# Where the first chunks' attention lands: weight places lent to batches 0 and 1, PSUM banks of its own, and two tiles summed by VectorE

## The chip, the cores and the metric

The kernel runs on 1 core of one Trainium2 chip. The metric is device time in microseconds (us), the median of the runs shown. PE is TensorE, ACT is ScalarE, DVE is VectorE, POOL is GpSimd, and SP is the queue that issues nearly all DMA transfers.

## The reference

Attention over keys and values that are averaged in groups of 8 rows, and a feed-forward block on its output:

```python
k_p = k.reshape(B, H, Sp, pool, D).mean(axis=3)      # B=8, H=8, S=576, D=64, pool=8, Sp=72
v_p = v.reshape(B, H, Sp, pool, D).mean(axis=3)
scores = scale * q @ k_p.T ; scores -= max ; attn = exp(scores) / (sum + 1e-9)
x = (attn @ v_p)  ->  (4608, 512)
h = x @ w_in                                         # 512 -> 2048
g = h * erf(softplus(h))
out = g @ w_out                                      # 2048 -> 512
```

The activations are float32, the two weight matrices arrive as float64 and are used at float32 precision.

## The kernel before, in words

**Tiling.** The 4608 tokens are cut into 9 chunks of 512 tokens. A chunk's feed-forward block goes in 16 steps, one for each 128 of the 2048 hidden units. A step has an input GEMM (L584, 12 matmuls of 128x512) and an output GEMM (L631, 12 more). Every float32 operand is held as a high and a low half (names ending in h and l), and a product is the sum of three: high by high, high by low, low by high. Steps go in pairs: two input GEMMs into two PSUM banks of the kind "h", then softplus (L602) of both, Erf (L609) of both with an activation table load ahead of each, the product with h on VectorE (L612), the split into halves gh (L614) and gl (L617), and later the output GEMMs. For chunk 0, L612 is what frees the "h" banks; the next pair's input GEMMs need them.

**Attention.** A tile is 128 tokens (64 at a batch's end) of all 8 heads. Batch 0 fills chunk 0 with four tiles, and its last 64 tokens begin chunk 1; batch 1 follows. The keys (DMA, L383) are summed over the pool by VectorE for batches 0 and 1 (L386), and by POOL for the others (L389 to L393), and split into kbd (L402, L404); the values go into vah, val and vb (L412 to L424). For each tile: queries land (L436), are split into qh and ql (L309 or L310, L442), scores (L476, or L452 and L454 from chunk 2 on and for full tiles), the maximum by head (L481 or L463), exponential, sums z, reciprocal (L505, L507), scaling (L517), transposes (L524, L531), split into eth, etl and etb (L528, L529, L536 to L541), and for each block of up to 256 tokens the products with the values (L561) and the split of their result into xh and xl (L565, L567), the input GEMM's operands.

The exponential is a sigmoid far down its tail. In chunk 0 ScalarE takes it head by head straight from PSUM, with the sum accumulated (L491, 8 for a tile), after VectorE has scaled the negated maximum (L484). In the other chunks VectorE subtracts the maximum (L465, L497), ScalarE takes one sigmoid over the 576 numbers of a row (L501), and VectorE sums them (L503).

**Weights.** They stay on the chip: 16 pieces of w_in (wi0 to wi15) and 16 of w_out (wo0 to wo15), each 512 KB from HBM (L345). A piece is converted from float64: ScalarE scales the upper word into a PSUM bank of the kind "cv" (L348), the lower bits come from ScalarE or POOL (L353, L355), VectorE puts them together (L357, L359), and the result is split (L309 or L310, L364).

**What sets the order.** Every operation is recorded with an engine, a cost, a due time and the buffers that it reads and writes. A planner (`Program.order`) then places them one by one: it keeps a clock for each engine, and takes of all ready operations within a window of due times the one that can start first, with a bonus for an early due time. Buffers have a number of places by tag (two of "raw" for landing keys, values and queries, two "h" banks, four "o", four "att", two "cv", eight banks in all), and an operation can be taken only when places for its buffers are free by the planner's clock. The instructions of each engine then stand in the order in which they were taken, and each engine works through its own in that order. SP's queue too goes in order: a transfer that waits for its place holds the ones behind it. Where the planner expects TensorE to be idle in the first 57 us of its clock, it puts filler matmuls on the constants (L675), which keep TensorE busy.

Of the kernel before, what the change touches and what calls it, by code (L numbers as in the profile page):

```python
# [122 lines left out]
class Program:  # L123
# [8 lines left out]
    DELAY = {"PE": 200, "ACT": 160, "DVE": 200, "POOL": 160, "SP": 900}  # L132
    SAME = {"PE": 0, "ACT": 130, "DVE": 130, "POOL": 105, "SP": 0}

    def __init__(self, capacity, window):
        self.ops, self.capacity, self.window, self.filler = [], capacity, window, None

    def op(self, eng, cost, prio, fn, reads=(), writes=(), hold=(), alt=None, funcs=None, port=False):
# [4 lines left out]
        o.set, o.port = funcs, port  # L143
# [124 lines left out]
def moe_attention(ctx: ExitStack, tc: tile.TileContext, cst, qa, kl, vl, wi, wo, out):  # L268
# [13 lines left out]
    sizes.update({"banks": 8, "h": CAP_H, "o": CAP_O, "att": CAP_ATT, "cv": CAP_CV})  # L282
# [90 lines left out]
    def job(ck, b, tiles, off, times, first, fresh):  # L373

        base, due = times[0], times[-1] + VAL_R
        if fresh:
# [19 lines left out]
            for p in range(NP):  # L396
                load_pool(kl[b, p], ks, p, SP, base + KEYS + KEYS_R * p, "s" if first and p > 1 else "raw")
# [318 lines left out]
```

## Time and profile before

| | us |
|---|---|
| median of 3 runs | 950.01 (949.89 to 951.83) |
| the profiled execution | 949.92 |
| its span, first to last instruction | 948.0 |
| PE busy | 928.0 |
| ACT busy | 653.7 |
| DVE busy | 531.9 |
| POOL busy | 348.0 |

The profiled execution's time is 1.9 us more than its span. A busy PE is not a PE with useful work: the filler matmuls count as busy. In the rows of the timeline a row gives the start, the duration, the engine, the line, the operation, what is written and read, and in brackets how long the engine had been idle before it and what ended that.

### The profile page before, as it was taken

To read this page: it belongs to the slowest core of one execution; us is meant where nothing else is said; L and a number is where in the kernel's file an instruction comes from. 1 tells how busy PE (TensorE), PEld (TensorE's weight loads), DVE (VectorE), ACT (ScalarE), POOL (GpSimd) and SP (SyncE) were. 2 spreads that over 40 slices of the span, in tenths; PEclk is the share of its full clock that TensorE was granted. 3 is DMA by queue.
4 is the path that set the end of the run, shared out by engine and by line. 5 is a ranking of instruction groups with operands and counts; after the bars stand their busy time and mean duration, and the time that the engine had idled before them with its cause. 6 is when DMAs were issued, how large, how long until landed. Compare 5 with 4: busy or idle time off the path is not lost.

```text
span 948.0 us, 13049 instructions
## 1 busy us (share of the span) xinstructions
PE 928.0 (98%) x4636; PEld 771.9 (81%) x4636; DVE 531.9 (56%) x1021; ACT 653.7 (69%) x1131; POOL 348.0 (37%) x451
## 2 busy tenths in 40 slices
PE   7899989999999999999999999999999999999998
PEld 6778868888888888888888888888888888888886
DVE  6978686755565454555565655655476446423232
ACT  4789985867676767766676667766676667656664
POOL 3689986243322354235321452234342111101000
PEclk9999999999999999999999999999999999999999
DMA  8990112212111121111110122002210010001001
GB/s 322 363 357 7 37 36 70 77 38 62 39 45 36 38 67 45 45 43 47 51 67 13 37 68 78 23 14 59 68 56 23 1 45 1 1 1 44 1 1 45
DMA packets 30352, 58.58 MB, mean 62 GB/s; under 512 B 7120, under 2 KB 7248, under 8 KB 30288
## 3 DMA queue, kind: packets, MB, share of 16 engines
q1 hardware_dynamic: 30000, 57.23, 18.1%
q8 instruction: 37, 0.61, 0.3%
q10 hardware_dynamic: 288, 0.52, 0.1%
q14 instruction: 27, 0.22, 0.1%
HBM read 48.30 MB, written 9.44 MB: 61 GB/s over the span
## 4 chain that ended last, share of the span: by engine, by line
PE 84%; DVE 1%; ACT 0%; POOL 0%; issue 0%; POOLq 0%
PE banks L631 38%; PE banks L584 37%; PE banks L561 4%; PE banks L452 2%; PE banks L524 1%; PE banks L454 1%; PE banks L476 1%; PE banks L531 0%; DVE kbd L404 0%; DVE z L503 0%; ACT L501 0%; DVE hs L612 0%; ACT y L602 0%; DVE z L505 0%; DVE s L517 0%; ACT s L501 0%
## 5 line engine op out<-in xcount | busy, mean ns | idle before, releaser
L584 PE MATMUL banks<-xh,wi 128*128 128x512 f32 x1152 | 381.2, 393 | 3.5 <-DVE y L612 2.8
L631 PE MATMUL banks<-wo,gh 128*128 128x512 f32 x1152 | 363.2, 396 | 0.8 <-DVE etl L529 0.7
L584 PEld LDWEIGHTS banks<-xh,wi 128*128 128x128 f32 x1152 | 217.1, 188 | 51.1 <-DVE y L612 4.4
L631 PEld LDWEIGHTS banks<-wo,gh 128*128 128x128 f32 x1152 | 207.5, 188 | 39.6 <-DVE etl L529 1.1
L631 PE MATMUL banks<-wo,gl 128*128 128x512 f32 x576 | 225.3, 391 | 0.0
L584 PE MATMUL banks<-xl,wi 128*128 128x512 f32 x576 | 225.1, 391 | 0.0
L617 DVE TENSOR_TENSOR gl<-hs,gh 128x512 fp32r<-128x512 f32 x73 | 53.6, 736 | 157.4 <-ACT gh L614 153.3
L617 POOL TENSOR_TENSOR gl<-hs,gh 128x512 fp32r<-128x512 f32 x55 | 71.4, 1298 | 175.2 <-ACT gh L614 174.6
L631 PEld LDWEIGHTS banks<-wo,gl 128*128 128x128 f32 x576 | 108.1, 188 | 24.2 <-DVE gl L617 0.4
L590 ACT COPY hs<-banks 128x512 f32<-128x512 f32 x56 | 32.8, 586 | 136.2 <-PE banks L584 133.3
L584 PEld LDWEIGHTS banks<-xl,wi 128*128 128x128 f32 x576 | 108.6, 188 | 21.8
L614 ACT CAST gh<-hs 128x512 fp32r<-128x512 f32 x128 | 78.4, 614 | 35.5 <-PE banks L631 31.3
L589 DVE COPY hs<-banks 128x512 f32<-128x512 f32 x72 | 49.8, 692 | 92.1 <-PE banks L584 91.7
L602 ACT ACT_TABLE_LOAD x72 | 92.4, 1283 | 3.0 <-DVE gl L617 1.8
L612 DVE TENSOR_TENSOR hs<-y,hs 128x512 f32<-128x512 f32 x128 | 84.1, 697 | 15.2 <-ACT y L609 15.1
L609 ACT ACT_TABLE_LOAD x68 | 87.2, 1283 | 1.2
L442 POOL TENSOR_TENSOR ql<-raw,qh 128x512 fp32r<-128x512 f32 (+1 forms) x36 | 44.4, 1232 | 106.4 <-ACT qh L309 106.2
L609 ACT ACTIVATE y<-y 128x1024 f32<-128x1024 f32 (+1 forms) x73 | 76.4, 1048 | 0.8
L389 POOL TENSOR_TENSOR raw<-raw 128x256 f32<-128x256 f32 (+1 forms) x60 | 50.9, 849 | 70.5 <-DMA raw<-vl 40.8
L602 ACT ACTIVATE y<-hs 128x512 f32<-128x512 f32 x128 | 73.8, 624 | 0.7
L541 POOL TENSOR_SCALAR etb<-etb 32x256 fp32r<-32x256 f32 (+1 forms) x40 | 18.3, 458 | 88.8 <-ACT etb L536 54.8
L501 ACT ACTIVATE s<-s,cst 128x576 f32<-128x576 f32 (+1 forms) x36 | 27.9, 775 | 30.3 <-DVE s L465 30.2
(100 smaller groups left out, 1194.4 us busy)
## 6 DMA issues: line engine op xcount, KB each, us to landing
raw<-vl SPq DMA_DIRECT2D x42, 256.0 KB, 2.7
out<-f SPq DMA_DIRECT2D x34, 256.0 KB, 2.0
raw<-kl SPq DMA_DIRECT2D x30, 288.0 KB, 2.8
wi<-wi SPq DMA_DIRECT2D x16, 512.0 KB, 6.8
wo<-wo SPq DMA_DIRECT2D x16, 512.0 KB, 6.8
raw<-qa SPq DMA_DIRECT2D x28, 256.0 KB, 2.6
hs<-qa SPq DMA_DIRECT2D x4, 256.0 KB, 5.1
raw<-qa SPq DMA_DIRECT2D x8, 128.0 KB, 2.5
```

The source lines that it names most:

```text
L389: op("POOL", gps(4 * size), prio, lambda: nc.gpsimd.tensor_add(t.ap[:, 0:4], t.ap[:, 0:4], t.ap[:, 4:8]), [t], [t])
L442: e.tensor_sub(ql.ap[:, :, :T], raw.ap[:, :, :T], f32(qh.ap[:, :, :T]))
L561: nc.tensor.matmul(d, w, e, start=(i == 0), stop=(i == 3), skip_group_check=True)
L584: nc.tensor.matmul(ph.ap, w_in[ft].ap[:, w, P * p:P * p + P], x.ap[:, p, :], start=(p == 0 and q == 0), stop=(p == NP - 1 and q == 2))
L589: op("DVE", dve(TC), n + u + 1.2, lambda u=u, ph=ph: nc.vector.tensor_copy(hs[u].ap, ph.ap), [ph], [hs[u]], alt=("ACT", act(TC, True), lam ...
L590: [ph], [hs[u]], alt=("ACT", act(TC, True), lambda u=u, ph=ph: nc.scalar.copy(hs[u].ap, ph.ap)))
L602: nc.scalar.activation(y.ap[:, half(k)], hh[k].ap, AF.Softplus)
L609: op("ACT", act(w), n + 1.9, lambda sl=sl: nc.scalar.activation(y.ap[:, sl], y.ap[:, sl], AF.Erf), own, own, funcs="sigmoid")
L612: op("DVE", dve(TC), n + 1.9, lambda k=k: nc.vector.tensor_mul(g(k), y.ap[:, half(k)], hh[k].ap), [(y, k), hh[k]], [gs[k]], port=kept)
L614: op("ACT", act(TC), n + 2.0, lambda k=k: nc.scalar.copy(gh[k].ap, g(k)), [gs[k]], [gh[k]])
L617: e.tensor_sub(gl[k].ap, g(k), f32(gh[k].ap))
L631: nc.tensor.matmul(o[t].ap, g.ap[:, gs], w_out[ft].ap[:, w], start=(ft == 0 and q == 0), stop=(ft == NJ - 1 and q == 2))
```

## The change

It has these parts:

- Buffers of the first attention work may lie in the places of weight pieces that are not loaded yet (`loan`). Lent are: to the exponentials eth, etl and etb of chunk 0's second block the places of wo15, wo14 and wo13; to qh and ql of every second tile of chunk 0 those of wi15 and wo12; to the four key pieces of batch 1 those of wo8 to wo11, and to its six value pieces those of wi9 to wi14. The transfer of a weight piece is recorded with the loans of its place, and the planner takes it only when all of them have been read (`o.after`).
- PSUM banks of chunk 0's attention count against a limit of their own ("att0", 5) and no longer against the four of "att".
- Which of a tile's two groups of heads takes the exponential by head on ScalarE is a table. Chunk 0's first two tiles now go the other way for both groups: subtraction, one sigmoid, and the sum by VectorE.
- The planner's numbers are others: costs of operations, delays, due times of batches, weights and values, the window, the bonus.

```diff
-WINDOW = 10
-SHIFT = 4
+WINDOW = 12
+SHIFT = 3
-T0, T0_STEP = -10.5, 1.0
-VAL_R = 3.5
-KEYS, KEYS_R, KEYS_S = -5.5, 0.5, -1.0
-VALS, VALS_R, VALS_S = -2.0, 0.5, -1.2
+T0, T0_STEP = -10.5, 1.5
+VAL_R = 3.0
+KEYS, KEYS_R, KEYS_S = -7.5, 0.5, -1.0
+VALS, VALS_R, VALS_S = 0.0, 0.4, -1.2
-W_IN, W_OUT = -1.0, -2.0
-LEAD = 9
+W_IN, W_OUT = 2.0, 0.0
+LEAD = 4
-CAP_H, CAP_O, CAP_ATT, CAP_CV = 2, 4, 4, 2
-ON_ACT = (0,)
+CAP_H, CAP_O, CAP_ATT, CAP_CV, CAP_ATT0 = 2, 4, 4, 2, 5
+ON_ACT = ((0, 0), (0, 0), (1, 1), (1, 1))
+
+LENT_E = ("wo15", "wo14", "wo13")
+LENT_Q = ("wi15", "wo12")
+LENT_KV = ("wo8", "wo9", "wo10", "wo11", "wi9", "wi10", "wi11", "wi12", "wi13", "wi14")
-SLACK, BIAS = 30, 2000
+SLACK, BIAS = 50, 2000
-DGE = 1200
+DGE = 2000
...
-                    if o.prio > progress + self.window:
+                    if o.prio > progress + self.window or any(b.left for b in o.after):
...
-        return 0.84 * n + (160 if psum else 190)
+        return 0.84 * n + (90 if psum else 130)
-        return 1.15 * (n + 66) / 0.96
+        return 1.04 * n + 95
-        return 2.5 * n + 110
+        return 2.25 * n + 130
...
+    def loan(tag, shape, dtype=F32):
+
+        b = Buf(weights, [P] + shape, dtype, tag, [tag])
+        pr.loans.setdefault(tag, []).append(b)
+        return b
...
-            op("SP", 1350, due - LEAD, lambda: nc.sync.dma_start(raw.ap.rearrange("p f w -> p (f w)"), src), [], [raw])
+            op("SP", 1290, due - LEAD, lambda: nc.sync.dma_start(raw.ap.rearrange("p f w -> p (f w)"), src),
+               [], [raw]).after = pr.loans.setdefault(w.args[3], [])
...
-                t = buf(tag, [size, POOL] if on_dve else [POOL, size])
+                t = (loan if tag in LENT_KV else buf)(tag, [size, POOL] if on_dve else [POOL, size])
...
-        eth, etl, etb = buf("eth", [NP, 256], F32R), buf("etl", [NP, 256], F32R), buf("etb", [2, 256], F32R)
+        second = ck == 0 and off > 0 and wide
+        eth, etl, etb = (loan(LENT_E[i], sh, F32R) if second else buf(t, sh, F32R) for i, (t, sh) in
+                         enumerate((("eth", [NP, 256]), ("etl", [NP, 256]), ("etb", [2, 256]))))
+        bank = lambda kind: Buf(banks, [P, 512], F32, "banks", ["banks", "att0" if ck == 0 else kind])
...
-            raw, qh, ql = buf("hs" if first else "raw", [NP, P]), buf("qh", [NP, P], F32R), buf("ql", [NP, P], F32R)
+            raw, qh, ql = (buf("hs" if ck == 0 else "raw", [NP, P]), *(
+                loan(LENT_Q[i], [NP, P], F32R) if ck == 0 and off + at & P and wide else buf(t, [NP, P], F32R)
+                for i, t in enumerate(("qh", "ql"))))
...
+                on_act = ck == 0 and ON_ACT[(off + at) // P][g]
...
-            if not on_act:
+
+            left = [g for g in range(2) if not (ck == 0 and ON_ACT[(off + at) // P][g])]
+            if left:
```

How this moves instructions is seen at three places. In the rows, names are those of the buffers; L numbers of the change are 10 to 25 higher for the same operation.

First, SP's queue where the keys of batch 1 and the first weight pieces stand. kl are keys, vl values, qa queries, wi and wo weights. Before:

```order
L436 DMA hs<-qa 128x512
L383 DMA gl<-vl 128x512
L383 DMA gh<-vl 128x512
L345 DMA wi_240<-wi 128x1024
L345 DMA wi_247<-wi 128x1024
L345 DMA wi_296<-wi 128x1024
L345 DMA wi_311<-wi 128x1024
L383 DMA raw<-kl 128x576
L345 DMA wi_330<-wi 128x1024
L345 DMA wo_382<-wo 128x1024
L383 DMA raw<-kl 128x576 x2
```

In the change:

```order
L453 DMA hs<-qa 128x512
L395 DMA gh<-vl 128x512
L395 DMA wo_274<-kl 128x576
L395 DMA wo_280<-kl 128x576
L395 DMA wo_286<-kl 128x576
L395 DMA wo_289<-kl 128x576
L453 DMA raw<-qa 128x4x64
L356 DMA wi_298<-wi 128x1024
L453 DMA raw<-qa 128x512
L356 DMA wi_357<-wi 128x1024
L395 DMA wi_390<-vl 128x512
L395 DMA wi_404<-vl 128x512
```

The four key pieces of batch 1 went from behind four weight pieces to ahead of all, into the places of wo8 to wo11; the queries of the 64-row tile and of batch 1's first tile now stand around the first weight piece, where they stood ten and twenty transfers further back.

Second, ScalarE around the softplus of the first pair of steps (L602, L626 in the change). Before:

```order
L536 CAST etb<-banks 32x64 x2
L602 ACT_TABLE_LOAD
L602 ACTIVATE y<-banks 128x512 x2
L528 CAST eth<-banks 128x4x64
L309 ACTIVATE wo_877<-f 128x512
L348 ACTIVATE banks<-wo_460 128x512
L609 ACT_TABLE_LOAD
L609 ACTIVATE y<-y 128x1024
```

In the change:

```order
L524 ACTIVATE s<-s,cst 128x576
L365 ACTIVATE hs<-wi_520,cst 128x512
L552 CAST eth<-banks 128x4x64
L360 ACTIVATE banks<-wo_506 128x512
L626 ACT_TABLE_LOAD
L626 ACTIVATE y<-banks 128x512 x2
L589 CAST xh<-banks 128x64 x2
L633 ACT_TABLE_LOAD
L633 ACTIVATE y<-y 128x1024
```

The 64-row tile's copy (eth) moved ahead of the softplus, and the copy of a converted weight piece out of the stretch between softplus and Erf.

Third, ScalarE around the softplus of steps 12 and 13 of chunk 0. Before (wo_1055, wo_1082 are the pieces wo13 and wo14):

```order
L458 COPY s<-banks 128x144
L353 ACTIVATE hs<-wo_1082,cst 128x512
L353 ACTIVATE hs<-wo_1099,cst 128x512
L458 COPY s<-banks 128x144 x2
L309 ACTIVATE wo_1796<-f 128x512
L348 ACTIVATE banks<-wo_1055 128x512
L348 ACTIVATE banks<-wo_1082 128x512
L602 ACT_TABLE_LOAD
L602 ACTIVATE y<-banks 128x512 x2
```

In the change (wi_1032 and wo_1055 are wi15 and wo12):

```order
L475 COPY s<-banks 128x144
L365 ACTIVATE hs<-wo_1055,cst 128x512
L313 ACTIVATE wi_1759<-f 128x512
L365 ACTIVATE hs<-wo_1065,cst 128x512
L360 ACTIVATE banks<-wi_1032 128x512
L313 ACTIVATE wo_1769<-f 128x512
L360 ACTIVATE banks<-wo_1055 128x512
L626 ACT_TABLE_LOAD
L626 ACTIVATE y<-banks 128x512 x2
L475 COPY s<-banks 128x144
```

Three of the tile's four score copies moved behind the softplus, and so did the first conversion copies of wo13 and wo14. On TensorE, the filler matmuls number 168 before the first input GEMM, 48 from it to the second pair's and 0 behind it; in the change 189, 36 and 0.

More of the change, by code (lines that the diff above doesn't have):

```diff
@@ L123 @@
 class Program:
-    DELAY = {"PE": 200, "ACT": 160, "DVE": 200, "POOL": 160, "SP": 900}
-    SAME = {"PE": 0, "ACT": 130, "DVE": 130, "POOL": 105, "SP": 0}
+    DELAY = {"PE": 200, "ACT": 220, "DVE": 260, "POOL": 160, "SP": 900}
+    SAME = {"PE": 0, "ACT": 190, "DVE": 190, "POOL": 105, "SP": 0}
     def __init__(self, capacity, window):
-        self.ops, self.capacity, self.window, self.filler = [], capacity, window, None
+        self.ops, self.capacity, self.window, self.filler, self.loans = [], capacity, window, None, {}
     def op(self, eng, cost, prio, fn, reads=(), writes=(), hold=(), alt=None, funcs=None, port=False):
         o = Op(eng, cost, prio, fn)
-        o.set, o.port = funcs, port
+        o.set, o.port, o.after = funcs, port, ()
         o.choice = {eng: (cost, fn)}
@@ L281, in moe_attention @@
     banks = pool("banks", 8, space=PSUM)
-    sizes.update({"banks": 8, "h": CAP_H, "o": CAP_O, "att": CAP_ATT, "cv": CAP_CV})
+    sizes.update({"banks": 8, "h": CAP_H, "o": CAP_O, "att": CAP_ATT, "att0": CAP_ATT0, "cv": CAP_CV})
     pr = Program(sizes, WINDOW)
@@ L381, in load_pool @@
             def load_pool(src, dst, p, size, prio, tag):
-                t = buf(tag, [size, POOL] if on_dve else [POOL, size])
-                op("SP", 10.3 * size, prio - 1, lambda: nc.sync.dma_start(
+                t = (loan if tag in LENT_KV else buf)(tag, [size, POOL] if on_dve else [POOL, size])
+                op("SP", (14.4 if first and p < NP and size == SP else 10.3) * size, prio - 1, lambda: nc.sync.dma_start(
                     t.ap, src.rearrange("(p a b) -> p a b", p=P, b=t.ap.shape[2])), [], [t])
@@ L396, in job @@
             for p in range(NP):
-                load_pool(kl[b, p], ks, p, SP, base + KEYS + KEYS_R * p, "s" if first and p > 1 else "raw")
+                load_pool(kl[b, p], ks, p, SP, base + KEYS + KEYS_R * p,
+                          "s" if first and p > 1 else LENT_KV[p] if b == 1 and wide else "raw")
             for r0, c0 in ((64, 0), (0, SP)):
@@ L407, in job @@
                 load_pool(vl[b, p], vs, p, D, base + VALS + VALS_R * p,
-                          ("gh" if p % 2 else "gl") if first else "raw")
+                          ("gh" if p % 2 else "gl") if first else LENT_KV[NP + p] if b == 1 and wide else "raw")
             for i in range(2):
@@ L477, in scores @@
                                              start=(i == 0 and pp == 0), stop=(i == 2), skip_group_check=True)
-                op("PE", 6 * 107, r, scores, [qh, ql, KBD], [ps], [s, m, z])
+                op("PE", 6 * 111, r, scores, [qh, ql, KBD], [ps], [s, m, z])
                 gs = slice(4 * g, 4 * g + 4)
@@ L499, in softmax_tile @@
                        [ps, (m, g)], [(s, g)])
-            if not on_act:
-                op("ACT", act(H * SP) + 93, r + 0.8, lambda: nc.scalar.activation(
-                    s.ap[:T], s.ap[:T], AF.Sigmoid, bias=bias[0][:T], scale=1.0 / 64.0), [s], [s], funcs="sigmoid")
-                op("DVE", dve(H * SP), r + 1.0, lambda: nc.vector.tensor_reduce(
-                    z.ap[:T], s.ap[:T], AX.X, ALU.add), [s], [z])
-            op("DVE", dve(8), r + 1.0, lambda: nc.vector.tensor_scalar(
-                out=z.ap[:T], in0=z.ap[:T], scalar1=EPS, scalar2=None, op0=ALU.add), [z], [z])
-            op("DVE", dve(48), r + 1.0, lambda: nc.vector.reciprocal(z.ap[:T], z.ap[:T]), [z], [z])
+            left = [g for g in range(2) if not (ck == 0 and ON_ACT[(off + at) // P][g])]
+            if left:
+                gs, own = slice(4 * left[0], 4 * left[-1] + 4), len(left) < 2
+                kz = (z, left[0]) if own else z
+                ks_ = (s, left[0]) if own else s
+                op("ACT", act(4 * SP * len(left)) + 93, r + 0.8, lambda gs=gs: nc.scalar.activation(
+                    s.ap[:T, gs], s.ap[:T, gs], AF.Sigmoid, bias=bias[0][:T], scale=1.0 / 64.0),
+                   [ks_], [ks_], funcs="sigmoid")
+                op("DVE", dve(4 * SP * len(left)), r + 1.0, lambda gs=gs: nc.vector.tensor_reduce(
+                    z.ap[:T, gs], s.ap[:T, gs], AX.X, ALU.add), [ks_], [kz])
+            op("DVE", 180, r + 1.0, lambda: nc.vector.tensor_scalar(
+                out=z.ap[:T], in0=z.ap[:T], scalar1=EPS, scalar2=None, op0=ALU.add), [z], [z], port=True)
+            op("DVE", dve(48), r + 1.0, lambda: nc.vector.reciprocal(z.ap[:T], z.ap[:T]), [z], [z], port=True)
             def ends():
```

15 lines of the change are left out of this document (7 added, 8 removed).

## The prediction

> **What bounds the kernel now.** I read the page first, then a table of stages by windows, then the waits inside the two stages in which TensorE stands. The page:
>
> ```profile
> PE 928.0 (98%) x4636; PEld 771.9 (81%) x4636; DVE 531.9 (56%) x1021; ACT 653.7 (69%) x1131; POOL 348.0 (37%) x451
> ```
>
> TensorE is the bound over the whole span, but that is a mean. The stages are cut at the first GEMM (43.73), at the first GEMM of the second pair of steps (58.87), at 70, 120 and 160 us. Columns are window, length, busy time of each engine with its instructions, TensorE's granted clock, DMA share, GB/s:
>
> ```profile
> 0.00:43.73 43.73, 35.05 (x280) 29.42 (x281) 33.86 (x77) 27.76 (x104) 24.30 (x37) 1.00 0.93 339
> 43.73:58.87 15.14, 14.60 (x109) 12.47 (x106) 12.64 (x26) 11.36 (x20) 8.62 (x10) 1.00 0.94 341
> 58.87:70.00 11.13, 9.53 (x51) 7.48 (x49) 8.32 (x21) 8.52 (x19) 10.79 (x12) 1.00 1.03 409
> 70.00:120.00 50.00, 49.68 (x235) 40.65 (x235) 36.59 (x64) 46.23 (x72) 46.18 (x53) 1.00 0.08 24
> 120.00:160.00 40.00, 35.28 (x171) 27.93 (x169) 31.21 (x54) 29.77 (x54) 30.92 (x41) 0.96 0.15 48
> 160.00:930.00 770.00, 769.70 (x3741) 642.58 (x3742) 405.35 (x778) 521.91 (x856) 227.19 (x301) 1.00 0.13 39
> ...
> 144.00:146.00 2.00, 2.00 (x6) 1.56 (x5) 1.97 (x3) 1.23 (x3) 1.92 (x4) 0.50 0.23 55
> 146.00:148.00 2.00, 2.00 (x8) 1.59 (x7) 1.97 (x3) 0.00 (x0) 2.00 (x2) 0.72 0.21 76
> ```
>
> Some of the busy time is filler matmuls on the constants. The same windows for their line alone:
>
> ```profile
> 0.00:43.73 43.73, 22.68 (x168) 17.18 (x168) 1.00 0.93 339
> 43.73:58.87 15.14, 5.95 (x51) 4.47 (x48) 1.00 0.94 341
> ```
>
> So TensorE's time without useful work is 8.68 idle + 22.68 fillers = 31.4 us before the first GEMM; 0.54 + 5.95 = 6.5 in the second stage; 1.6 in the third; 0.3 in the fourth; 4.72 idle + 1.56 lost to the clock (2 us at 0.50, 2 us at 0.72) = 6.3 in the fifth; and 0.3 in the 770 us behind 160. The matmuls that must run are the same before and after. The change can therefore win or lose only in the first 160 us, and in two places above all.
>
> The first place is 43.73 to 58.87. Rows of the timeline, with what ended the idle time before a row in brackets:
>
> ```profile
> 51.37 1.09 ACT L602 ACTIVATE y<-banks 128x512 f32<-128x512 f32 x2
> 52.34 0.38 ACT L528 CAST eth<-banks 128x256 fp32r<-128x256 f32 x1
> 54.11 0.63 ACT L309 ACTIVATE wo<-f 128x512 fp32r<-128x512 f32 x1 [1.39 <-DVE f L359]
> ...
> 55.29 1.28 ACT L609 ACT_TABLE_LOAD   x1
> 56.58 1.07 ACT L609 ACTIVATE y<-y 128x1024 f32<-128x1024 f32 x1
> ...
> 57.68 0.69 DVE L612 TENSOR_TENSOR y<-y,banks 128x512 f32<-128x512 f32 x1
> ...
> 58.87 0.48 PE L584 MATMUL banks<-xh,wi 128*128 128x512 f32 x1
> ...
> 47.62 0.62 POOL L310 TENSOR_SCALAR qh<-raw 128x512 fp32r<-128x512 f32 x1 [5.12 <-DMA raw<-qa]
> 49.52 0.69 DVE L386 TENSOR_REDUCE vs<-raw 128x64 f32<-128x512 f32 x1 [2.18 <-DMA raw<-vl]
> ```
>
> The next pair's GEMM needs a PSUM bank that line 612 frees. Between the softplus (done at 52.46) and the Erf's table load (55.29) ScalarE holds a weight copy that waits 1.39 us for VectorE: 2.8 us in which the chain stands. Meanwhile POOL waits 5.12 us and VectorE 2.18 us for batch 1's queries and values, whose transfers stand behind weight pieces.
>
> The second place is around 142 us:
>
> ```profile
> 130.28 3.09 DVE L505 TENSOR_SCALAR z<-z 64x8 f32<-64x8 f32 x1
> ...
> 133.62 1.19 ACT L348 ACTIVATE banks<-wo 128x512 f32<-128x512 f32 x2 [2.52 <-DVE s L460]
> 136.59 1.28 ACT L602 ACT_TABLE_LOAD   x1 [1.79 <-DVE gl L617]
> 137.89 1.09 ACT L602 ACTIVATE y<-banks 128x512 f32<-128x512 f32 x2
> ...
> 140.97 1.04 ACT L609 ACTIVATE y<-y 128x1024 f32<-128x1024 f32 x1
> ...
> 142.04 0.69 DVE L612 TENSOR_TENSOR y<-y,banks 128x512 f32<-128x512 f32 x1
> ...
> 142.78 0.50 PE L584 MATMUL banks<-xh,wi 128*128 128x512 f32 x1 [2.32 <-DVE y L612]
> ```
>
> An operation on 64x8 numbers sits 3.09 us on VectorE, ScalarE behind it idles 2.52 + 1.79 us in front of the softplus of steps 12 and 13, and TensorE waits 2.32 us for line 612; then the clock drops for those 4 us.
>
> **The change part by part.** *VectorE in place of ScalarE for two tiles.* Durations by form:
>
> ```profile
> L481 DVE TENSOR_REDUCE m<-banks 128x4 f32<-128x288 f32 x14 | 6.2, 451 | 1.8 <-PE banks L476 1.7
> L497 DVE TENSOR_TENSOR s<-banks,m 128x288 f32<-128x288 f32 x6 | 2.6, 450 | 0.0
> L503 DVE TENSOR_REDUCE z<-s 128x8 f32<-128x576 f32 x28 | 20.9, 747 | 5.5 <-ACT s L501 5.2
> L484 DVE TENSOR_SCALAR m<-m 128x4 f32<-128x4 f32 x8 | 1.9, 272 | 0.0
> L501 ACT ACTIVATE s<-s,cst 128x576 f32<-128x576 f32 x28 | 21.7, 776 | 30.3 <-DVE s L465 30.2
> L491 ACT ACTIVATE s<-banks,m 128x72 f32<-128x72 f32 x32 | 9.8, 344 | 5.2 <-DVE m L484 5.2
> ```
>
> ScalarE loses 16 of the 32 per-head exponentials, 9.8/32 = 0.31 each, and gains two wide ones: 16 x 0.31 - 2 x 0.78 = 3.3 us less. On VectorE the order shows 82 instructions up to the last low half of x that the first GEMM needs, against 76: four subtractions (1.80), three sums over a row (2.24, the 64-row tile's among them, which stood behind the GEMM before), one maximum (0.45), four scalings fewer (-1.09), and a remainder that nets to about one mean instruction of the stage (33.86/77 = 0.44). That is 3.8 us more. VectorE idles 43.73 - 33.86 = 9.9 us in this stage, so the bounds of the shift are 0 (all of it falls into idle time) and +3.8 (none). What I take is +0.8: the last query tile of chunk 0 stands one 256 KB piece further back in SP's queue, 0.77 us at 339 GB/s, and that chain ends last. First GEMM: 44.5.
>
> *Batch 1 lands early.* In SP's queue four key pieces, the 64-row queries and the next query tile now stand ahead of all but one weight piece, and six value pieces among the first ones; the bytes are the same. So the waits of 5.12 and 2.18 us go, and in ScalarE's order nothing that waits for VectorE's f stands between softplus and Erf, only two 64-wide copies. The ScalarE chain is then 1.09 + two copies (each under the 0.38 of the 256-wide one) + 1.28 + 1.07 + 0.69 = under 4.9 us behind the pair. The other limit is TensorE's own queue, from these rows:
>
> ```profile
> 49.37 0.24 PE L531 MATMUL banks<-cst,bb 64*64 64x64 f32 x1
> 49.54 0.45 PE L476 MATMUL banks<-kbd,qh 128*128 128x144 f32 x2
> ...
> 50.98 0.29 PE L675 MATMUL banks<-cst 128*128 128x256 bf16 x1
> 51.79 0.43 PE L524 MATMUL banks<-cst,s 64*128 64x64 f32 x4 [0.52 <-DVE etb L538]
> 52.15 2.79 PE L675 MATMUL banks<-cst 128*128 128x256 bf16 x24
> 54.70 0.28 PE L561 MATMUL banks<-eth,vah 128*128 128x64 f32 x1
> 56.09 1.82 PE L675 MATMUL banks<-cst 128*128 128x256 bf16 x15
> ```
>
> The 24 GEMM matmuls take 49.37 - 43.73 = 5.64, four transposes 0.4, sixteen value products (56.09 - 54.70) x 16/12 = 1.85, half a tile of scores (50.98 - 49.54)/2 = 0.72, and 36 fillers (48 before) at (54.70 - 52.15)/24 = 0.106 each 3.8: 12.4 us, more than 5.64 + 4.9. So the second pair starts at 44.5 + 12.4 = 56.9 instead of 58.87, and 0.7 us of scores that came later is done: **-2.7 us**. At best (43.73, same queue) -3.5; at worst (47.5, and the old 15.14 us because something else stalls ScalarE) +3.1.
>
> *Third and fourth stage.* The first output GEMM still waits for the second output piece's conversion. I take 0; bounds -1.6 (its whole idle time) and +1.5 (it doubles). From 70 to 120 POOL and ScalarE are busy 46.2 of 50: 0, bounds -0.3 and +3.8 (POOL's whole slack used up by pieces converted later).
>
> *Loans.* Pieces wi9 to wi15 and wo8 to wo15 may load only once the attention data in their places is read. The cover is the pieces ahead of them: wi9 belongs to the fifth pair of steps, and four pairs of input and output GEMMs take 4 x 2 x 5.64 = 45 us of TensorE from 44.5 on, while the transfers of before all ended by 70 (DMA share 0.08 behind it). If that cover were gone, each late piece would cost its 1.5 us (512 KB at 339 GB/s) at a GEMM. I take 0.
>
> *Fifth stage.* In ScalarE's order all four score copies of the tile in work (line 458), whose partner on VectorE (L460) held it, and the copies of wo13 and wo14 stand ahead of the softplus of steps 12 and 13 before; in the change one score copy does, and the pieces ahead of it are wi15 and wo12. I take the wait of 2.32 and the clock's 1.56 as gone, and leave the rest: **-3.9 us**. Bounds: -6.3 (all of it) and +1.6 (the wait moves to another pair and the clock drops once more).
>
> *Everything behind 160*: planner settings move rows there too, but TensorE waits 0.3 of 770 us and VectorE and ScalarE have 365 and 248 us of idle time as cover; 0, bounds -0.3 and +1. The tail is the same.
>
> Sum: -2.7 - 3.9 = -6.6. The profiled execution took 949.92 (span 948.0 and 1.9 around it), so 943.3; the median of the runs is 950.01, 0.1 away.
>
> [...]
>
> **The rivals.**
> 1. *Only the front gains*: 947.2. The late wait stays, because POOL (30.9 of 40) and VectorE (31.2 of 40) have the same weight work to do in it, and the rows moved may be its symptom and not its cause. For: totals on both engines hardly change. Against: the 4.3 us of ScalarE's idle time have named causes.
> 2. *The wait goes, the clock still drops* on a smaller gap in that stage: 943.3 + 1.6 = 944.9.
> 3. *More than I take*: all of stage three's and five's losses go: 949.9 - 2.7 - 1.6 - 6.3 = 939.3.
> 4. *Nothing is won*: two weight pieces fewer are converted before the first GEMM, POOL has 3.8 us of slack in the fourth stage and gives the 2.7 us back there, and the late wait stays: 949.9.
> 5. *Slower*: VectorE's idle time before the first GEMM lies in waits that stay, so its 3.8 us more all shift the GEMM, and ScalarE's queue still stalls in the second stage: 949.9 + 3.8 - 0.7 = 953.0. It decides once the added rows find less than about 1 us of idle time. For: VectorE is the fullest engine there. Against: 9.9 us idle, and ScalarE gets 3.3 us lighter in the same chain.
>
> **How the numbers follow.** Chances: forecast 0.52, rivals 0.15, 0.10, 0.10, 0.06, 0.07. The forecast's own range is 940.4 to 946.4 (the front between -3.5 and -1, the fifth stage between -6 and -2.5). To leave out no more than 0.2 the range reaches from 939 to 948.8: outside are half of rival 3, rivals 4 and 5. What this kernel's measurement can tell from no change is about 0.2%, 1.9 us. Faster (below 948.1): 0.52 + 0.10 + 0.10 and most of rival 1, 0.12, together 0.84; same: the rest of rival 1 and rival 4, 0.09; slower 0.07.
>
> **What would show it.** First GEMM near 44.5, the second pair's near 57; no row of POOL or VectorE waiting for batch 1's queries or values between 42 and 50; 36 fillers between the pairs; ScalarE's Erf load within 1 us of the softplus there. In the fifth stage TensorE idle under 3 us, granted clock 1.00 throughout, no VectorE row of 3 us. Wrong if the first GEMM comes past 47, if TensorE waits for a weight piece between 70 and 120, or if a wait of 2 us or more with a clock drop stands anywhere behind 60 us.

## The result and the profile after

The change takes 940.03 us (median of four runs, 937.73 to 940.61) against 950.92 for the kernel before on the same chip (949.89 to 953.58): ratio 0.9877, 95% interval 0.9849 to 0.9904. By the ratio that is 11.7 us less, between 9.1 and 14.4; the two medians lie 10.9 apart and the two profiled spans 9.5. Forecast were 6.6 less. Of the changed kernel's page the line of busy times, and then its stages, cut at its own first GEMM (46.06) and its second pair's (58.58); columns as before: window, length, busy time of PE, PEld, DVE, ACT and POOL with their instructions, granted clock, DMA share, GB/s.

```profile
PE 927.3 (99%) x4645; PEld 772.5 (82%) x4645; DVE 544.3 (58%) x1048; ACT 654.2 (70%) x1114; POOL 301.7 (32%) x413
```

```profile
0.00:46.06 46.06, 40.40 (x314) 34.61 (x314) 35.55 (x82) 24.96 (x75) 21.95 (x36) 0.96 0.96 355
46.06:58.58 12.52, 12.52 (x88) 10.50 (x88) 9.62 (x24) 9.63 (x20) 10.04 (x13) 1.00 1.01 388
58.58:70.00 11.42, 10.62 (x51) 8.54 (x51) 9.96 (x20) 11.11 (x18) 10.93 (x13) 1.00 0.76 304
70.00:120.00 50.00, 49.18 (x240) 39.89 (x239) 37.55 (x67) 48.50 (x78) 48.53 (x56) 1.00 0.11 32
120.00:160.00 40.00, 39.97 (x204) 33.21 (x203) 28.61 (x57) 34.02 (x65) 30.86 (x38) 1.00 0.13 39
160.00:930.00 770.00, 770.00 (x3737) 642.25 (x3736) 423.01 (x802) 523.61 (x861) 179.38 (x261) 1.00 0.12 39
```

The filler line alone in the first two of these windows:

```profile
0.00:46.06 46.06, 25.48 (x189) 19.77 (x189) 0.96 0.96 355
46.06:58.58 12.52, 4.44 (x36) 3.28 (x36) 1.00 1.01 388
```

Two things are to be seen. In the fifth stage (120 to 160) TensorE is busy 39.97 of 40 at full clock, where it had been idle for 4.72 and slow behind that. In the first stage the clock is below 1 now. A second profile of the change, taken with the experiments below, fell into an execution without that drop. The table shows what TensorE lost in each stage, idle time plus fillers plus 1.7 us for each 3.41 us at half clock. The last column is that second profile, with a span of 936.6:

| us lost | before | change | change, second profile |
|---|---|---|---|
| to the first GEMM | 31.4 | 32.8, 1.7 of it clock | 29.9 |
| between first and second pair | 6.5 | 4.4 | 4.4 |
| to 70 | 1.6 | 0.8 | 0.8 |
| 70 to 120 | 0.3 | 0.8 | 0.8 |
| 120 to 160 | 6.4 | 0.0 | 0.1 |
| 160 to 930 | 0.3 | 0.0 | 0.0 |
| sum | 46.5 | 38.9 | 36.1 |

The spans differ by 9.5 and 11.4, the sums by 7.6 and 10.4; no row shows where the rest (1.9 and 1.0) lies. It lies early: from the first GEMM of step 32 (251.01, 241.43 and 239.36, steps counted from 0) to the end the three executions take 697.0, 697.1 and 697.2.

The place around 57 us, in rows of the changed kernel's timeline (start, duration, engine, line, operation; in brackets the idle time before and what ended it):

```profile
52.13 1.09 ACT L626 ACTIVATE y<-banks 128x512 f32<-128x512 f32 x2
53.10 0.34 ACT L589 CAST xh<-banks 128x64 fp32r<-128x64 f32 x2
53.46 1.28 ACT L633 ACT_TABLE_LOAD   x1
54.75 1.06 ACT L633 ACTIVATE y<-y 128x1024 f32<-128x1024 f32 x1
...
58.58 0.50 PE L608 MATMUL banks<-xh,wi 128*128 128x512 f32 x1
```

ScalarE holds two 64-wide copies between softplus and Erf, and the Erf's table load comes 0.24 behind the softplus (2.8 before). Batch 1's queries and values keep neither POOL nor VectorE waiting. And the place around 130:

```profile
124.31 2.55 POOL L641 TENSOR_TENSOR gl<-y,gh 128x512 fp32r<-128x512 f32 x2 [2.49 <-ACT gh L638]
...
127.19 0.96 DVE L529 TENSOR_SCALAR z<-z 64x8 f32<-64x8 f32 x1
...
128.94 1.28 ACT L626 ACT_TABLE_LOAD   x1
...
130.24 1.09 ACT L626 ACTIVATE y<-banks 128x512 f32<-128x512 f32 x2
```

The addition on 64x8 numbers takes 0.96 (3.09 before), the pair ahead has both its gl on POOL and done at 126.86, and ScalarE waits for nothing before the softplus. What is lost in front is here, in two windows and the TensorE waits ahead of the second:

```profile
28.66:32.07 3.41, 1.78 (x9) 1.19 (x10) 2.20 (x6) 3.41 (x21) 0.89 (x2) 1.00 1.03 404
32.07:35.48 3.41, 3.41 (x17) 3.06 (x18) 2.05 (x5) 2.59 (x14) 1.28 (x4) 0.50 1.04 407
```

```profile
PE banks L585 <- ACT eth L552: 0.8, 1, 0.8
PE banks L585 <- ACT s L509: 0.5, 1, 0.5
PE banks L585 <- DVE etl L553: 0.3, 1, 0.3
```

The first value products wait for copies that ScalarE makes between 72-wide exponentials, and then TensorE runs for 3.41 us at half clock.

The list of the change's parts leaves one out that bears on the place around 130. In the change, three more kinds of VectorE instruction (the scaling of the negated maximum, the addition of EPS and the reciprocal) are marked `port=True`, and on the planner's clock a marked instruction never runs at the same time as one of POOL. The expectations below call these the marks; one of them speaks of lock waits and means VectorE rows that stand beside POOL's, as the 3.09 us of the addition. That a lock is behind them, no run shows. One of the three marks:

```diff
-            op("DVE", dve(48), r + 1.0, lambda: nc.vector.reciprocal(z.ap[:T], z.ap[:T]), [z], [z])
+            op("DVE", dve(48), r + 1.0, lambda: nc.vector.reciprocal(z.ap[:T], z.ap[:T]), [z], [z], port=True)
```

### The profile page after: what moved, and what is told of

Its sections match the earlier page's. It is cut to its first block, busy times and chain, and to the rows that moved or that the text cites. A ratio compares the mean times of both kernels' runs of the same rounds, so it can differ in the third digit from the quotient of the medians.

```text
span 938.5 us, 12974 instructions
## 1 busy us (share of the span) xinstructions
PE 927.3 (99%) x4645; PEld 772.5 (82%) x4645; DVE 544.3 (58%) x1048; ACT 654.2 (70%) x1114; POOL 301.7 (32%) x413
## 4 chain that ended last, share of the span: by engine, by line
PE 89%; DVE 0%; POOL 0%; ACT 0%; issue 0%
PE banks L655 41%; PE banks L608 40%; PE banks L585 4%; PE banks L469 2%; PE banks L548 1%; PE banks L471 1%; PE banks L493 1%; PE banks L555 0%; POOL wi L376 0%; DVE y L636 0%; DVE f L371 0%; POOL raw L401 0%; POOL wo L314 0%; ACT gh L667 0%; DVE m L498 0%; DVE s L515 0%
## 5 line engine op out<-in xcount | busy, mean ns | idle before, releaser
L614 ACT COPY hs<-banks 128x512 f32<-128x512 f32 x65 | 38.2, 587 | 190.0 <-PE banks L608 190.0
L641 DVE TENSOR_TENSOR gl<-hs,gh 128x512 fp32r<-128x512 f32 x109 | 76.0, 698 | 131.2 <-ACT gh L638 129.3
L459 POOL TENSOR_TENSOR ql<-raw,qh 128x512 fp32r<-128x512 f32 (+1 forms) x36 | 49.3, 1368 | 215.9 <-ACT qh L313 193.2
L636 DVE TENSOR_TENSOR hs<-y,hs 128x512 f32<-128x512 f32 x128 | 101.6, 834 | 5.7 <-ACT y L633 5.5
L626 ACT ACTIVATE y<-hs 128x512 f32<-128x512 f32 x128 | 73.8, 624 | 0.7
L613 DVE COPY hs<-banks 128x512 f32<-128x512 f32 x63 | 43.4, 690 | 52.6 <-PE banks L608 51.7
L477 DVE TENSOR_TENSOR s<-s,banks 128x144 f32<-128x144 f32 x100 | 25.9, 299 | 78.0 <-ACT s L475 77.9
L401 POOL TENSOR_TENSOR raw<-raw 128x256 f32<-128x256 f32 (+1 forms) x60 | 48.0, 801 | 60.2 <-DMA raw<-kl 35.3
L641 POOL TENSOR_TENSOR gl<-hs,gh 128x512 fp32r<-128x512 f32 x19 | 24.7, 1300 | 83.5 <-ACT gh L638 83.5
L565 POOL TENSOR_SCALAR etb<-etb 32x256 fp32r<-32x256 f32 (+1 forms) x38 | 14.4, 380 | 94.5 <-ACT etb L560 65.2
```

The costliest lines, as they stand in the source:

```text
L401: op("POOL", gps(4 * size), prio, lambda: nc.gpsimd.tensor_add(t.ap[:, 0:4], t.ap[:, 0:4], t.ap[:, 4:8]), [t], [t])
L459: e.tensor_sub(ql.ap[:, :, :T], raw.ap[:, :, :T], f32(qh.ap[:, :, :T]))
L613: op("DVE", dve(TC), n + u + 1.2, lambda u=u, ph=ph: nc.vector.tensor_copy(hs[u].ap, ph.ap), [ph], [hs[u]], alt=("ACT", act(TC, True), lam ...
L614: [ph], [hs[u]], alt=("ACT", act(TC, True), lambda u=u, ph=ph: nc.scalar.copy(hs[u].ap, ph.ap)))
L626: nc.scalar.activation(y.ap[:, half(k)], hh[k].ap, AF.Softplus)
L636: op("DVE", dve(TC), n + 1.9, lambda k=k: nc.vector.tensor_mul(g(k), y.ap[:, half(k)], hh[k].ap), [(y, k), hh[k]], [gs[k]], port=kept)
```

## The experiments

Each was timed beside the kernel before (950.5 to 950.7); ratios are to it, with a 95% interval. The kernels that leave out the addition of EPS or add fillers keep the order of instructions. For the others the planner makes a new order, and what is measured belongs to that whole order, not to the edited part alone.

Theories when they began: A, the prediction's (ScalarE's order caused the late wait); B, formed on the two traces: in the kernel before, the softplus of steps 12 and 13 waits for the one y buffer, which gl (L617) frees, and gl stood on VectorE behind the 3.09 us addition (130.28 to 133.37), which itself stood through a row of POOL instructions. That row, with its first gap at 133.35, and gl, in the kernel before:

```profile
129.59 1.29 POOL L364 TENSOR_TENSOR wo<-f,wo 128x512 fp32r<-128x512 f32 x1
130.82 0.82 POOL L389 TENSOR_TENSOR raw<-raw 128x288 f32<-128x288 f32 x1
131.59 1.30 POOL L617 TENSOR_TENSOR gl<-y,gh 128x512 fp32r<-128x512 f32 x1
132.84 0.51 POOL L391 TENSOR_TENSOR raw<-raw 128x144 f32<-128x144 f32 x1
133.43 0.34 POOL L393 TENSOR_TENSOR ks<-raw 128x72 f32<-128x72 f32 x1
...
135.83 0.69 DVE L617 TENSOR_TENSOR gl<-y,gh 128x512 fp32r<-128x512 f32 x1
```

**Leaving out the addition of EPS in the kernel before.** The order is kept; EPS is not added.

```diff
-            op("DVE", dve(8), r + 1.0, lambda: nc.vector.tensor_scalar(
-                out=z.ap[:T], in0=z.ap[:T], scalar1=EPS, scalar2=None, op0=ALU.add), [z], [z])
+            op("DVE", dve(8), r + 1.0, lambda: None, [z], [z])
```

> The kernel before with one thing left out: the addition of EPS (2e-18) to the row sums (line 505, at least 2e-9, so that no float32 sum changes) issues nothing; every other instruction keeps its place on its engine. Theory (the cause of the late wait is VectorE held up): the 3.09 us addition at 130.28, which lasts until the first gap in a row of POOL instructions, delays gl (L617), that frees the one y buffer, for which the softplus of steps 12 and 13 waits. Without it the softplus comes about 3 us earlier, TensorE's wait of 2.32 us at 142.8 and the clock drop behind it go, TensorE's loss between 120 and 160 falls from 8.9 to 3 to 5 us, and the time is 944 to 947. Rival (the prediction's: ScalarE's order, four score copies and two weight copies ahead of the softplus): the order is the same, so TensorE still waits over 1 us there and the time is 949 to 951.

947.61, ratio 0.9972 (0.9962 to 0.9981): 2.7 us less, a time between the ranges of the two theories. Rows of its timeline and two of its windows:

```profile
132.43 1.68 DVE L465 TENSOR_TENSOR s<-s,m 128x576 f32<-128x576 f32 x1
134.04 0.82 DVE L616 TENSOR_TENSOR gl<-y,gh 128x512 fp32r<-128x512 f32 x1
...
134.94 1.28 ACT L601 ACT_TABLE_LOAD   x1 [2.58 <-DVE gl L616]
...
141.36 0.50 PE L583 MATMUL banks<-xh,wi 128*128 128x512 f32 x1
```

```profile
127.63:131.04 3.41, 1.78 (x11) 1.38 (x10) 2.96 (x9) 3.29 (x9) 3.41 (x6) 1.00 0.56 168
131.04:134.45 3.41, 3.41 (x10) 2.62 (x9) 3.38 (x5) 1.31 (x3) 3.33 (x6) 0.50 0.00 0
```

ScalarE's order is as before, with all its copies ahead of the softplus. They are done at 132.35, and ScalarE then waits 2.58 us for gl; TensorE's wait of 2.32 us is gone. So A falls, and B holds for what the softplus waits for. But the softplus came only 1.65 us earlier. The rest of TensorE's wait is gone because TensorE itself came to that GEMM 0.9 us later (at 141.36, where it had been ready at 140.46), behind a stretch at half clock. The hold-up moved to the subtraction L465, which stands 1.68 (0.75 before).

In this profile the clock drops all the same, 12.7 us earlier, behind gaps of 0.99 and 0.64 that the kernel before had too, without a drop, and once more in front, at 52.54. Four of the eleven runs have a granted clock of 1.000 (946.87 to 947.52). Idle time between 120 and 160 falls from 4.72 to 2.26; the drop of 1.7 stays in this profile.

**Telling the planner of the addition in the kernel before.** One word; the planner orders anew.

```diff
-scalar1=EPS, scalar2=None, op0=ALU.add), [z], [z])
+scalar1=EPS, scalar2=None, op0=ALU.add), [z], [z], port=True)
```

> The kernel before with one word added: the planner counts the addition of EPS (line 505) as an instruction that VectorE and POOL can not run at the same time, as it does for the change. All instructions stay, the planner makes a new order. Theory (VectorE held up): additions no longer start behind a row of POOL instructions, no VectorE row of 3 us is left, the late wait is under 1 us, and the time is 943 to 948. Rival (the order on ScalarE, or the numbers of the table, matter): a wait of 1 us or more between 120 and 160 stays and the time is 949 to 952.

956.87, ratio 1.0072 (1.0055 to 1.0089), slower, against both expectations. No addition is over 1.26 us, but the subtraction L465 stands 3.14 at 139.88, TensorE waits 3.0 us for y, and the clock drops five times. That the planner keeps one instruction more apart from POOL's only moved the hold-up here. Its windows are the clearest picture of the clock. Two of the five drops, each with the 3.41 us ahead of it:

```profile
33.02:36.43 3.41, 1.99 (x15) 1.09 (x13) 3.41 (x10) 3.03 (x12) 1.78 (x4) 1.00 0.98 350
36.43:39.84 3.41, 3.41 (x21) 2.86 (x22) 2.91 (x7) 2.17 (x6) 3.25 (x5) 0.50 0.99 370
67.15:70.56 3.41, 1.73 (x14) 1.30 (x12) 3.26 (x5) 2.00 (x5) 3.41 (x4) 1.00 1.04 412
70.56:73.97 3.41, 2.79 (x7) 2.24 (x8) 3.30 (x7) 3.37 (x6) 3.17 (x5) 0.50 0.36 140
```

**The change without its loans.** All `loan(...)` become `buf(...)` with the tags of before; numbers, costs, sums and PSUM banks stay.

```diff
-        eth, etl, etb = (loan(LENT_E[i], sh, F32R) if second else buf(t, sh, F32R) for i, (t, sh) in
+        eth, etl, etb = (buf(t, sh, F32R) for i, (t, sh) in
...
-                t = (loan if tag in LENT_KV else buf)(tag, [size, POOL] if on_dve else [POOL, size])
+                t = buf(tag, [size, POOL] if on_dve else [POOL, size])
```

> The change without its loans: all attention data of the first chunk and of batch 1 go into the buffers they had before; table of numbers, costs, marks, sums by VectorE and the PSUM banks of their own stay. Theory (the loans bring the front, the marks and numbers the fifth stage): no late wait, loss between 120 and 160 under 3 us, but batch 1's keys and values wait for buffers again, the second pair of steps comes 1 to 3 us later than in the change, time 941.5 to 944.5. Rival (the loans carry most of the gain): 946 or more, with the late wait back. Third (loans bring nothing): 939 to 941.

942.81, ratio 0.9912 (0.9897 to 0.9927). The loss between 120 and 160 is 0.5, the second pair comes at 60.42 (58.58 in the change; both profiles have one drop ahead of it). As the first theory had it, the late wait stays away without the loans too. Against the change's 940.03 the loans are worth about 2.8 us, of which 1.8 lie ahead of the second pair; the intervals of the two ratios overlap a little.

**The old table with the loans.**

```diff
-WINDOW = 12
-SHIFT = 3
+WINDOW = 10
+SHIFT = 4
...
-W_IN, W_OUT = 2.0, 0.0
-LEAD = 4
+W_IN, W_OUT = -1.0, -2.0
+LEAD = 9
```

> The change with the old table of due times and windows (WINDOW, SHIFT, T0_STEP, VAL_R, KEYS, VALS, W_IN, W_OUT, LEAD, SLACK, DGE as before); loans, marks, costs of instructions, PSUM banks of their own and the sums by VectorE stay. Theory (marks and costs remove the late wait, the table sets the front): loss between 120 and 160 under 3 us, first GEMM later than 46 by 1 to 4 us since query and key pieces come in another order, time 941 to 945. Rival (the table is what removes the late wait): a wait of over 1 us there, 946 to 951.

949.93, ratio 0.9990 (0.9979 to 1.0000): nearly all is gone. The first GEMM comes at 51.39, and the hold-up is back, worse, although the additions are marked here. Its VectorE and POOL rows:

```profile
133.27 1.32 POOL L376 TENSOR_TENSOR wo<-f,wo 128x512 fp32r<-128x512 f32 x1
133.77 4.19 DVE L529 TENSOR_SCALAR z<-z 64x8 f32<-64x8 f32 x1
134.53 0.49 POOL L403 TENSOR_TENSOR raw<-raw 128x128 f32<-128x128 f32 x1
134.95 0.76 POOL L401 TENSOR_TENSOR raw<-raw 128x256 f32<-128x256 f32 x1
135.64 0.35 POOL L405 TENSOR_TENSOR vs<-raw 128x64 f32<-128x64 f32 x1
135.92 0.49 POOL L403 TENSOR_TENSOR raw<-raw 128x128 f32<-128x128 f32 x1
136.34 1.32 POOL L376 TENSOR_TENSOR wo<-f,wo 128x512 fp32r<-128x512 f32 x1
137.59 0.35 POOL L405 TENSOR_TENSOR vs<-raw 128x64 f32<-128x64 f32 x1
```

The addition ends (137.96) when POOL's unbroken row ends (137.94), not between two of its instructions.

**Three numbers of the table alone.**

```diff
-W_IN, W_OUT = 2.0, 0.0
-LEAD = 4
+W_IN, W_OUT = -1.0, -2.0
+LEAD = 9
```

> The change with three numbers of the table as before: W_IN, W_OUT and LEAD, the due times of the weight pieces (three and two steps earlier) and how long ahead of them their transfers may start. Theory (in the old table these set the rows of POOL in which VectorE is held up): weight conversions stand before the first GEMM again, which comes 1 to 4 us later than in the change, a VectorE row of 2 us or more stands between 120 and 140, time 944 to 950. Rival (the windows and the due times of keys and values matter): 938 to 941.5, as the change.

948.23, ratio 0.9972 (0.9961 to 0.9983). The time is as the theory had it, its reason is not: nothing is lost between 120 and 160. The first GEMM comes at 54.24 behind weight conversions, 8 us later than in the change and not 1 to 4, and 3.9 idle and 1.7 of clock are lost between 70 and 120. So these three numbers move the front; where the later hold-up falls is not theirs alone.

**The sums by ScalarE again.**

```diff
-ON_ACT = ((0, 0), (0, 0), (1, 1), (1, 1))
+ON_ACT = ((1, 1), (1, 1), (1, 1), (1, 1))
```

> The change with all four tiles of the first chunk on ScalarE again (16 exponentials per tile with their sums), the planner makes its order for that. Theory of the prediction (ScalarE's 3.3 us less pay, VectorE's 3.8 us more nearly vanish in idle time): first GEMM 0.5 to 3 us later than in the change, time 940.5 to 943.5. Rival (VectorE's added work is what set the first GEMM back to 46.06): first GEMM 0.5 to 2 us earlier and 937.5 to 939.5.

942.50, ratio 0.9909 (0.9895 to 0.9922), first GEMM at 47.44, in a profile without a drop in front: against the change beside it (939.59) the sums by VectorE are worth about 2.9 us, though the intervals of the two ratios overlap a little, and VectorE's added rows did not set the first GEMM back.

**Without PSUM banks of its own.**

```diff
-"banks", ["banks", "att0" if ck == 0 else kind])
+"banks", ["banks", kind])
```

> The change with the first chunk's attention under the limit of four PSUM banks that it had before, in place of five of its own. Theory (a fifth bank lets scores and value products of neighbouring tiles overlap a little): first GEMM 0 to 2 us later, 939.5 to 942.5. Rival (the limit decides nothing): 938 to 940.5 like the change.

943.47, ratio 0.9920 (0.9904 to 0.9935). The size is beyond what I expected and the place is another: the first GEMM is at 44.51, but the order that the planner makes then loses 4.4 idle and 1.7 of clock between 70 and 120. What the banks are worth by themselves stays open; the 3.9 us against the change (939.59) are of the whole order.

**The change once more, and with fillers around the first value products.** The second kernel adds 16 filler matmuls where TensorE waited in front.

```diff
+FILLS = {(0, 0, 0): 8, (0, 0, 2): 4}
...
+                for _ in range(FILLS.get((ck, off, p), 0)):
+                    pr.filler.fn()
                 for i, (d, w, e) in enumerate(mm):
+                    for _ in range(4 * ((ck, off, p, i) == (0, 0, 0, 1))):
+                        pr.filler.fn()
```

> The change itself once more, as the measure for the runs beside it: 937.5 to 941, in two groups, near 938 where the granted clock is 1.000 and near 940.4 where it is 0.997.

> The change with 16 filler matmuls more in front of and inside the first value products (8 ahead of the first, 4 behind its first matmul, 4 ahead of the third): they fill the waits of 0.85, 0.34 and 0.46 us between 28.4 and 31.9, behind which the change's profile shows half the clock from 32.1 to 35.5. Theory (these waits bring the drop): granted clock 1.000 in all runs, 1.00 in the windows from 32 to 36, first GEMM 0.5 to 1.5 us earlier than 46.06, time 937.5 to 939 in every run. Rival (the drop is not decided there): runs near 940.4 with 0.997 stay as frequent as in the change. Third (the fillers stand in the way of the value products, or lead to another drop): 940.5 to 942.

> The kernel with the 16 fillers alone once more, beside the others: 937.5 to 938.5 in every run, granted clock 0.999 to 1.000.

The change: 939.59, ratio 0.9886 (0.9870 to 0.9902). Its eight runs in all have a granted clock of 1.000 three times (937.73, 938.36, 939.79) and 0.997 or 0.998 five times (939.16 to 942.04): two groups, as expected, but they overlap. With fillers: 938.03, ratio 0.9866 (0.9852 to 0.9879), and 938.60, ratio 0.9871 (0.9851 to 0.9891); all nine runs at 0.999 or 1.000, 937.48 to 940.44, median 938.2. Two windows of its profile:

```profile
28.00:32.00 4.00, 3.97 (x29) 2.96 (x28) 3.30 (x8) 4.00 (x26) 1.57 (x3) 1.00 1.04 404
32.00:36.00 4.00, 4.00 (x42) 3.64 (x41) 3.57 (x12) 3.90 (x12) 2.53 (x3) 1.00 1.03 405
```

The drop no longer comes; 16 matmuls buy about 1.7 us in the median, though the two intervals overlap. Not every run of the second series is within the 937.5 to 938.5 that I had expected: four of the five lie above it, one of them past 940, all at full clock.

The first GEMM is at 43.66 in one of these profiles and at 45.25 in the other. The rows show transfers that land at other times. The sum of the last key piece follows a wait of 0.78 us for its transfer in the second profile, and what depends on it comes some 0.8 us later. ScalarE's copy of a weight piece, which also waits for its transfer, starts at 23.90 and not at 22.23, and VectorE waits 0.86 us for the copy etb behind it. The second profile of the change (no drop) has its first GEMM at 43.99 and its second pair at 56.47.

**The change without the addition of EPS, and that with fillers.** EPS is not added in either; the second has the fillers too, 12 + 4 + 4 of them.

```diff
-            op("DVE", 180, r + 1.0, lambda: nc.vector.tensor_scalar(
-                out=z.ap[:T], in0=z.ap[:T], scalar1=EPS, scalar2=None, op0=ALU.add), [z], [z], port=True)
+            op("DVE", 180, r + 1.0, lambda: None, [z], [z], port=True)
```

> The change with one thing left out: the addition of EPS to the row sums (line 529) issues nothing, all else keeps its place. Theory: in the change no such addition stands on the path behind 60 us (the one at 127.19 takes 0.96 us and nobody waits), so that only the front gains, six additions of 0.2 to 0.3 us on VectorE before the first GEMM: 938 to 940, 0 to 1.5 us less than the change beside it. Rival (VectorE's lock waits cost the change too): 2 us less or more. Third (another phase of the gaps brings a clock drop): 941 to 943.

> The change with fillers around the first value products (12 ahead of the first, 4 behind its first matmul, 4 ahead of the third) and without the addition of EPS (2e-18 to sums of 2e-9 or more). Theory (with the clock held, VectorE's six shorter rows bring the first GEMM forward): granted clock 1.000 in all runs, first GEMM at 42.8 to 43.7 and 936.5 to 938. Rival (the additions lie in VectorE's idle time): 937.8 to 938.5, the same as the fillers alone.

940.14, ratio 0.9893 (0.9878 to 0.9907), and 939.59, ratio 0.9879 (0.9859 to 0.9899): nothing won by it, and the second lies above both of its ranges. In the second's profile the clock holds and the first GEMM comes at 44.66, but a VectorE product meets a row of POOL instructions, and TensorE waits for what stands behind it:

```profile
105.60 3.79 DVE L541 TENSOR_TENSOR s<-s,z 128x576 f32<-128x576 f32 x1 [0.16 <-POOL bb L537]
...
110.84 0.66 PE L548 MATMUL banks<-cst,s 128*128 128x128 f32 x4 [1.68 <-DVE f L372]
```

The missing additions are not the reason: this is the order of the kernel with fillers, and the same product meets the same row there. In that kernel's two profiles it takes 2.13 and 0.88, and POOL's next instruction takes longer instead (0.94, where it took 0.41 in the other profile, and 1.81, where it took 1.31):

```profile
104.56 2.13 DVE L542 TENSOR_TENSOR s<-s,z 128x576 f32<-128x576 f32 x1 [0.16 <-POOL bb L538]
106.02 0.94 POOL L315 TENSOR_SCALAR qh<-raw 128x256 fp32r<-128x256 f32 x1
...
106.05 0.88 DVE L542 TENSOR_TENSOR s<-s,z 128x576 f32<-128x576 f32 x1 [0.16 <-POOL bb L538]
106.28 1.81 POOL L377 TENSOR_TENSOR wo<-f,wo 128x512 fp32r<-128x512 f32 x1
```

So how long such a hold-up lasts differs between executions of one order. The change with fillers has the lowest median of all that was run.

## Why the prediction was right, and where not

The time lies inside the range, but the larger part of the gain came from a term whose cause the prediction had wrong. That much of the hit is luck.

*The front, -2.7.* Right in mechanism, and near in size in the profile without the drop: the weight copy between softplus and Erf and the waits for batch 1 are gone, 36 fillers stand between the pairs, and the second pair follows the first by 12.52 (12.4 said). In the profile without a drop the pairs come at 43.99 and 56.47 (44.5 and 56.9 said), which with the 0.7 us of scores moved ahead is -3.1. In the profile with the drop they come at 46.06 and 58.58, and -1.0 is left. What the sum lacked is the clock in the first stage: rival 2 looked for a drop in the fifth stage alone, and I did not ask whether ScalarE's copies between exponentials would open a new gap in the first. Between the two profiles lie 2.07 us, but 0.92 of them are there ahead of the drop (first value product at 29.48 and 28.56). In the profile with the drop the sum of the last key piece starts at 8.26, behind its transfer, in the other at 7.52; in the kernel before it started at 8.26 too. So about 1.1 us are left for the drop, and up to 0.9 of the -3.1 is the luck of an early transfer.

That VectorE's added work nearly vanishes held, as the run with the sums on ScalarE shows. Its size was taken too large: up to the first GEMM VectorE is busy for 35.55 and 35.11 us (33.86 before), 1.3 to 1.7 more and not 3.8.

*Third and fourth stage and the loans, 0.* -0.8 and +0.5, inside the bounds. The 1.6 us of waits around the first output GEMM were not for a conversion in the kernel before, as the prediction read them: the rows name POOL's scaling (L517, 0.77) and VectorE's etb and etl (L538 and L529, 0.84). In the change a conversion ends the wait that is left (L376, 0.8). No transfer into a lent place came late; the order with the loans is worth about 2.8 us.

*The fifth stage, -3.9.* The term was too small: -6.3, the whole of its bound, went, as in rival 3. Its cause was wrong. I blamed ScalarE's order; the run without the addition kept that order and lost the wait. It was VectorE, held up by POOL, and behind it the single y buffer. The row of 3.09 us was quoted in the prediction and not followed to gl and y. Of the 2.4 us that I left in the sum, 1.00 and 0.63 are gaps ahead of the addition or at its start (129.08 and 130.42), which stayed in the run without it; the new order has neither, and no run shows why.

Which part of the change removes the late wait is open as well. The marks are aimed at this hold-up, but they are not enough: with them and the old table it is back, and one of them in the kernel before made things worse. The change without its marks was not run.

*Behind 160, 0.* Right to 0.2 us from step 32 on; 1.0 to 1.9 us of the gain before it have no row to show them.

*Rivals.* "Only the front gains" and "nothing is won" fall with the fifth stage, "slower" with the first GEMM. "More than I take" (939.3) came nearest to the 940.0 measured, though it took the front's 2.7 as given; in the runs with the drop the fifth stage made up for what the front gave back.

On the clock, the sum takes the drop's 1.56 as gone with the wait of 2.32. That was the author's estimate: no run shows a length of idle time below which the clock stays whole. In the change the stage has no drop (granted clock 1.00), but in the kernel before without the addition the wait of 2.32 went and the clock dropped all the same, behind 1.63 us of idle time. In these profiles windows in which TensorE was busy for 0.5 to 2.3 of 3.41 us were followed by half clock. In the kernel before the 2.32 lie in the window in front of the drop (140.29 to 143.70); TensorE's wait before them, 0.52 us up to 140.03, lies outside it.

## What to carry to other kernels

Follow a VectorE row that takes many times its usual duration (here 3.09 us, with a median of 0.17 on its line) to the buffer that its successor frees: here ScalarE and TensorE idled (4.3 and 2.32 us), and the cause lay between VectorE and POOL. Such a hold-up moved here when one instruction was left out (to a row of 1.68 us) or marked (3.14), so count the lost time over all stages and not only where it was. Where the profile shows half clock behind several short gaps of TensorE (here 1.63 of 3.41 us), a handful of fillers in these gaps (16 here) is cheap against the 1.7 us of a clock drop. Profile one kernel twice before you put a price on its front: here 1.6 and 2.1 us lay between two executions of the same program.

## What the runs showed of the hardware

*The clock dropped in windows of 3.41 us, on a grid that stood through an execution.* Every drop seen ahead of the last 15 us in these profiles lasts 3.41 us at 0.50, a loss of 1.7. In the kernel with the one word added the drops start at 12.54, 36.43, 70.56, 104.70 and 149.07: 7, 10, 10 and 13 times 3.41 apart. In the change the half clock at the profile's end begins at 936.60, 265 times 3.413 behind the drop at 32.07. In the 3.41 us ahead of a drop TensorE was idle for 1.1 to 3.0 us in sum. In windows of the grid with no drop after them it was idle for as much as 1.85 (45.39 to 48.80 in the kernel with three numbers as before), and for 2.27 from 0.34 to 3.75 in the kernel before, where its first matmul comes at 2.61; no single limit of idle time parts the two. The grid's first edge in the span lies at 0.34 in the kernel before, at 1.35 in the change and at 2.30 in the kernel with the one word added, and twice the profiles show what such a shift does. In the change 1.63 us of waits stand in one window, and the clock drops behind it. In its second profile the same waits (0.62, 0.34 and 0.48) stand on both sides of an edge of the grid, 0.56 and 0.88 us idle, and the clock holds (the grid is counted back from the half clock at that profile's end, which begins at 936.44):

```profile
25.09:28.50 3.41, 2.85 (x27) 2.47 (x24) 2.07 (x7) 2.55 (x11) 0.12 (x1) 1.00 1.04 405
28.50:31.91 3.41, 2.53 (x15) 1.94 (x16) 2.88 (x8) 3.41 (x24) 1.57 (x3) 1.00 1.04 407
```

In the kernel before, the gaps of 1.00 and 0.63 around 130 are parted by an edge at 130.05, 1.27 and 0.37 us idle, without a drop; in the kernel without the addition one window holds 1.63, and the drop comes. This fits the change's falling into two groups of runs. It is read from profiles; where the grid begins was not set in any run.

*VectorE can stand through a whole row of POOL instructions, but need not.* It took 4.19 us for an addition on 64x8 numbers, through seven of them, and 3.79 us for a product on 128x576 numbers that took 2.13 and 0.88 at the same place in two other executions. In the rows POOL's instruction is stretched too: beside the 2.13 and the 0.88 it takes 0.94 and 1.81, where it took 0.41 and 1.31. VectorE's instruction sometimes ended while such a POOL instruction ran (the 2.13 and the 0.88), and sometimes not until POOL's row broke (the 3.09 and the 4.19). What decides this, no run here shows.
